# The first 512-token chunk of an attention-and-MLP kernel: ScalarE's first instructions, VectorE's and ScalarE's orders, and TensorE's first products rearranged

## The chip, the cores and the metric

One core of a Trainium2 chip runs the kernel. The metric is device microseconds of that core for one launch. The core has TensorE (PE in the profile; its weight loads are PEld), VectorE (DVE), ScalarE (ACT), GpSimd (POOL) and SyncE (SP), which issues most of the transfers. SP and ACT each have a transfer queue of their own (q1 and q10 in the profile); all queues share 16 DMA engines.

## What is computed

The input x has 2048 tokens of 1024 features, in bfloat16. It is normalised per token, goes through a dilated local attention (32 heads of 32, 8 keys at a distance of 2) and through a gated MLP with 3584 hidden features, and the two are combined:

```python
xn = _layernorm(x, axis=-1)
s = _A_ref(xn, A_wqkv, A_wo)      # qkv = xn @ wqkv; 8 keys at distance 2; softmax; @ wo
g = _silu(_B_ref(xn, B_w1, B_w3, B_w2))   # (silu(xn @ w1) * (xn @ w3)) @ w2
return x + s * g
```

## The kernel before

Tokens are worked in four chunks of 512 (c = 0 to 3), two chunks to a block (b = 0, 1); a chunk has four rows of 128 tokens (st = 0 to 3). The products of a block are done by a Strassen-like scheme of seven products on halves of the two chunks and halves of the features, so that sums of inputs and of weights on VectorE take the place of some products on TensorE.

**A planner orders everything but TensorE.** The kernel's body only records operations in a `Plan`: engine, name, what is read and written, an estimated duration. TensorE's operations stay in the order in which they are recorded. For the other engines `simulate` (L130) runs a list schedule with those estimates: whenever an engine is free it takes, of the operations ready by then, the one with the smallest `limit`. `limits` (L109) derives that from when TensorE needs the result; `plan.soon` lowers it by name; `plan.rank` replaces it by a fixed place for named operations of the start. The instructions are then emitted in the order found. Each engine runs its own in that order, and real waits are by semaphore. A transfer's estimate goes through one pipe with `plan.rate` bytes per microsecond, whatever queue issues it.

**The start.** Ahead of the plan, 19 products on a tile of zeros (`warm`, L296) are queued on TensorE, each 128x512. Then, for chunk 0:

- `x_load` (L371) brings the four rows of x, 256 KB each: rows 0 and 1 are issued by SP, rows 2 and 3 by ACT (names x0_0 to x0_3). SP goes on with wqkv0_0 and wqkv0_1 (two halves of the query weights, 1 MB each), four rows of chunk 1, and wqkv1_0, wqkv1_1.
- "warm" on ACT (L1155) is a square root on a dummy, so that its function table is loaded early.
- `ln_dve` (L379) normalises rows 0, 1 and 3 on VectorE: two statistics (bn0_0_0, bn0_0_1 for row 0, L385), their merge (ba0_0, L388), a square root on ACT (sq0_0, L390), a reciprocal on VectorE (rc0_0, L392) and the scaling (ts0_0, L393). `ln_act` (L397) normalises row 2 on ACT: mean0_2 (L404), var0_2 (L409), sq0 (L413), then rc0 and nm0 on VectorE (L416, L417), then nrm0_2 (L421).
- `ln_tp` (L425) transposes a normalised row on TensorE by eight products with an identity, four for each half of the features (L434), and an eviction brings each half from PSUM to `xT` (L441; xT0_0_0 and xT0_0_1 are the halves of row 0). All evictions of chunk 0 are on ACT.
- `qkv_first` (L518) with `rows0` (L1179) makes the first query products as soon as a row is there: for each row 16 products of 128 columns on wqkv0_0 and the first half of that row's features (L311). They need xT0_st_0 alone. `fill` (L1171) puts products on zeros into the order to bridge a wait; they write a bank that the first products of row 0 overwrite.

TensorE's order at the start is: transposes of row 0; fill of 5; transposes of row 1; products of row 0; transposes of row 2; products of row 1; transposes of row 3; products of row 2; products of row 3. After that come `fsnap`, copies of the four banks by ACT, and 16 products on wqkv0_1 and the second halves (called fc11 here, from the name of their evictions), then the same for the key weights, between which the rows of chunk 1 are transposed (tp1_0 to tp1_3).

Chunk 1's normalisation (bn1_0_0 and so on) is ranked behind chunk 0's. `attention` (L615) of a chunk runs on VectorE, beside the MLP's products: logits into E; transfers L of E; sums z; maximum and sum trees tr; zd; exp on ACT; rec; pb; transfers E back; then the weighted sum of values. For chunk 3 alone `plan.soon` lowers the limits of L, z, tr, zd, exp, rec, pb and E by 200 us.

Of the kernel before, what the change touches and what calls it, by code (L numbers as in the profile page):

```python
# [14 lines left out]
PE, DVE, ACT, POOL, SP = range(5)  # L15
# [14 lines left out]

class Op:
    __slots__ = ("eng", "emit", "rd", "wr", "occ", "lat", "table", "nbytes", "pred", "succ", "n",
                 "start", "done", "ready", "limit", "name", "late", "idx", "rate")


class Plan:
# [3 lines left out]
    def __init__(self):  # L40
        self.ops, self.slots, self.pools = [], [], {}
        self.shift = 0.0
        self.rate = 3e5
        self.rank, self.soon = {}, {}

    def slot(self, pool, name):
        s = Slot(self, pool, name)
# [1 line left out]
        self.slots.append(s)  # L49
        return s  # L50

    def op(self, eng, name, emit, rd=(), wr=(), occ=0.0, lat=0.08, table=None, nbytes=0, late=0.0):
        o = Op()
        o.eng, o.name, o.emit, o.rd, o.wr, o.occ, o.lat = eng, name, emit, list(rd), list(wr), occ, lat
        o.table, o.nbytes, o.late, o.idx, o.rate = table, nbytes, late + self.shift, len(self.ops), self.rate
        for c in o.rd + o.wr:
            s = c[0] if isinstance(c, tuple) else c
            if isinstance(s, Slot):
                if s.first is None:
                    s.first = o.idx  # L60
                s.last = o.idx
        self.ops.append(o)
        return o
# [45 lines left out]
    def limits(self):  # L109
        t = 0.0  # L110
        for o in self.ops:
            o.limit = None
            if o.eng == PE:
                o.limit = t
                t += o.occ
        for o in reversed(self.ops):
            lim = [self.ops[s].limit - self.hop(o, self.ops[s]) for s in o.succ]
            lim = min(lim) if lim else t
            d = o.occ + o.lat
            if o.nbytes:  # L120
                d = o.occ + 2.6 + o.nbytes / o.rate
            lim -= d
            o.limit = lim if o.limit is None else min(o.limit, lim)
            o.limit += o.late
        for o in self.ops:
            o.limit += self.soon.get(o.name, 0.0)
            if o.name in self.rank:
                o.limit = self.rank[o.name] - 1000.0

    def simulate(self):  # L130
        ops = self.ops
        free = [0.0] * 5
        ready = [[] for _ in range(5)]
        pes = [o.idx for o in ops if o.eng == PE]
        pe_at = 0
        table = None
        pipe = 0.0
        for o in ops:
            o.n, o.ready = len(o.pred), 0.0
            o.start = None  # L140
        for o in ops:
            if not o.n:
                ready[o.eng].append(o.idx)
        left = len(ops)
        order = []
        while left:
            best = None
            for e in reversed(range(5)):
                if e == PE:
                    if pe_at == len(pes) or ops[pes[pe_at]].n:  # L150
                        continue
                    T = max(free[PE], ops[pes[pe_at]].ready)
                elif ready[e]:
                    T = max(free[e], min(ops[i].ready for i in ready[e]))
                else:
                    continue
                if best is None or T < best[0]:
                    best = T, e
            T, e = best
            if e == PE:  # L160
                o = ops[pes[pe_at]]
                pe_at += 1
            else:
                i = min((i for i in ready[e] if ops[i].ready <= T), key=lambda i: (ops[i].limit, i))
                ready[e].remove(i)
                o = ops[i]

            occ = o.occ
            if o.table and o.table != table:
                occ += 1.29  # L170
                table = o.table
            o.start = T
            free[e] = T + occ
            if o.nbytes:
                pipe = max(pipe, T + occ + 0.9) + o.nbytes / o.rate
                o.done = pipe + 1.3
            else:
                o.done = T + occ + o.lat
            left -= 1
            order.append(o)  # L180
            for s in o.succ:
                q = ops[s]
                q.n -= 1
                q.ready = max(q.ready, o.done + self.hop(o, q))
                if not q.n and q.eng != PE:
                    ready[q.eng].append(s)
        self.order = order
        return order
# [13 lines left out]
def kernel(  # L202
# [101 lines left out]
    def mm(ps, lhs, rhs, first, rd, last=True, mark=(), st=None):  # L304

        n = len(lhs)
        cut = (lambda a: a) if st is None else (lambda a: a[:, st * P:(st + 1) * P])

        def emit():
            for k in range(n):  # L310
                nc.tensor.matmul(  # L311
                    cut(ps.ap()), lhsT=lhs[k](), rhs=cut(rhs[k]()), start=(first and k == 0),
                    stop=(last and k == n - 1), skip_group_check=not (first and last) or st is not None,
                )

        plan.op(PE, "mm " + ps.name, emit, rd, [ps] + list(mark), n * (MM if st is None else TP), 0.0)
# [11 lines left out]
        plan.op(ACT, name, lambda: nc.scalar.activation(out=o(), in_=a(), func=ACTF.Silu), rd, wr, occ, 0.11,  # L328
                table="silu")

    def dma(eng, name, o, a, rd, wr, kb, late=0.0):
        e = {SP: nc.sync, POOL: nc.gpsimd, ACT: nc.scalar}[eng]
        occ = {SP: 0.45, POOL: 0.58, ACT: 0.55}[eng]
        plan.op(eng, name, lambda: e.dma_start(out=o(), in_=a()), rd, wr, occ, 0.0, nbytes=kb * 1024, late=late)  # L334

    def sub_of(s, *idx):
        return (s,) + idx
# [33 lines left out]
    def x_load(c, st, xt, eng=SP):  # L371
        g = c * NST + st
        dma(eng, f"x{c}_{st}", lambda: xt.ap().rearrange("p (s d) -> p s d", s=NST)[:, st, :],
            lambda: x_flat[g * P:(g + 1) * P, :], [], [(xt, st)], 256)

    def xrow(xt, st):
        return xt.ap().rearrange("p (s d) -> p s d", s=NST)[:, st, :]
# [85 lines left out]
    def qkv_w(wt, k, j):  # L463
        return lambda: wt.ap().rearrange("p (k c j) -> p k j c", k=4, j=NJ)[:, k, j, :]
# [53 lines left out]
    def qkv_first(nm, wts, mid=None, rows=None):  # L518

        pa = [bank(f"f{nm}{j}") for j in range(4)]  # L520
        for st in range(NST) if rows else ():
            rows(st, pa[0])
            for j in range(4):
                mm(pa[j], [qkv_w(wts[0], k, j) for k in range(KH)], bx[0, 0], st == 0, [wts[0]] + xt_cells(0, 0, st),
                   st=st)
        for j in range(4):
            if mid is not None and j != 2:
                mid(min(j, 2))
            if not rows:
                mm(pa[j], [qkv_w(wts[0], k, j) for k in range(KH)], bx[0, 0], True, [wts[0]] + xt_cells(0, 0))  # L530
            dst, wr = first_at(nm, j)
            cp("fsnap", dst, pa[j].ap, [pa[j]], wr)
        for j in range(4):
            if mid is not None and j == 0:
                mid(3)
            mm(pa[j], [qkv_w(wts[1], k, j) for k in range(KH)], bx[0, 1], False, [wts[1]] + xt_cells(0, 1))
            dst, wr = home(0, nm)(j)
            cp("fc11", dst, pa[j].ap, [pa[j]], wr)
# [609 lines left out]
        pend.append(tail)  # L1148


    x0, x1 = plan.slot("r8", "x0"), plan.slot("r8", "x1")
    plan.rate = 3.3e5
    for st in range(NST):
        x_load(0, st, x0, ACT if st > 1 else SP)
    plan.op(ACT, "warm", lambda: nc.scalar.activation(out=scr[:], in_=eps_t[:], func=ACTF.Sqrt), [], [], 0.2,  # L1155
            table="sqrt")
    plan.rank = {n: i for row in (
# [3 lines left out]
    ) for i, n in enumerate(row.split())}  # L1161
    for st in range(NST):
        for n in ("bn1_%d_0", "bn1_%d_1", "ba1_%d", "sq1_%d", "rc1_%d", "ts1_%d", "xT1_%d_0"):
            plan.rank[n % st] = len(plan.rank)
# [1 line left out]
    for st in range(NST):  # L1166
        if st == 2:
            ln_act(0, [2], x0)
        else:
            ln_dve(0, st, x0, [("seq", 0, 0)] if st == 1 else [])  # L1170
    def fill(ps, n):  # L1171

        def emit():
            for _ in range(n):
                nc.tensor.matmul(ps.ap(), lhsT=warm[:, 0:P], rhs=warm[:, 0:CH], start=True, stop=True)

        plan.op(PE, "fill", emit, [], [ps], n * MM, 0.0)

    def rows0(st, ps):  # L1179
        if st == 0:  # L1180
            ln_tp(0, 0, x0)
            fill(ps, 5)
            ln_tp(0, 1, x0)
        elif st < NST - 1:
            ln_tp(0, st + 1, x0, (ACT, ACT))

    plan.shift = 0.0
    for b in range(NB):
# [58 lines left out]
    attention(3)  # L1247
    wo(3, wots, last=t4_last)
    flush()
    plan.soon = {n + "3": -200.0 for n in ("L", "z", "tr", "zd", "exp", "rec", "pb", "E")}  # L1250
    plan.run()


# [28 lines left out]
```

## Time and profile before

| what | value |
|---|---|
| three runs | 720.35, 720.47, 720.61 us; median 720.47 |
| the profiled execution, its own time | 720.51 us |
| its span, first to last instruction | 718.7 us |
| what lies around the span | 1.8 us |
| PE busy | 710.5 us (99%), 3329 products |
| PEld, DVE, ACT, POOL busy | 344.6, 642.0, 385.6, 50.2 us |
| transfers | 150.55 MB, mean 209 GB/s |
| granted TensorE clock | 9 of 9 in all 40 slices |

The chain that ended last gives PE 98% of the span. "Busy" of PE counts the products on zeros too, and the end of each product is modelled: a 128x512 product is listed with 379 ns, while a stream of them starts every 0.216 us. Where rows are merged, the first number is the start of the first instruction, the second the time to the end of the last. A bracket at the end of a row is how long the engine had been idle, and what ended that.

### The profile page before, as it was taken

How to read it: one execution, taken by the hardware profiler on the slowest of the kernel's cores; microseconds unless marked ns; L12 is line 12 of the kernel's file. 1: busy time of each engine (PE TensorE's matmuls, PEld its weight loads, DVE VectorE, ACT ScalarE, POOL GpSimd, SP SyncE). 2: the span in 40 equal slices, each digit the busy share in tenths (PEclk: the TensorE clock that was granted, in tenths of full speed). 3: DMA queues.
4: the chain of work that ended last, by engine and by line, in shares of the span. 5: the costliest groups of instructions: out<-in, count | busy, mean ns of one | idle time of the engine just before them, and what ended most of it. 6: DMA issues, size and time to landing. Idle time of an engine off the chain costs nothing.

```text
span 718.7 us, 9254 instructions
## 1 busy us (share of the span) xinstructions
PE 710.5 (99%) x3329; PEld 344.6 (48%) x3384; DVE 642.0 (89%) x861; ACT 385.6 (54%) x655; POOL 50.2 (7%) x102
## 2 busy tenths in 40 slices
PE   9999999999999999999999999999999999999997
PEld 5655544444444444444555554444444444444443
DVE  6997999988999999589999999776999995899935
ACT  7754466576555799242535354676565654412133
POOL 0020100202000000202000000201000002200000
PEclk9999999999999999999999999999999999999999
DMA  9589895878644849884554559887537347655502
GB/s 337 191 293 387 285 335 162 265 204 242 210 138 165 287 148 227 247 243 122 186 164 157 175 197 318 266 292 236 185 114 252 111 155 213 212 196 171 175 30 88
DMA packets 128589, 150.55 MB, mean 209 GB/s; under 512 B 13856, under 2 KB 105504, under 8 KB 124192
## 3 DMA queue, kind: packets, MB, share of 16 engines
q1 hardware_dynamic: 113728, 121.13, 52.6%
q0 software_dynamic: 6080, 26.22, 10.4%
q10 hardware_dynamic: 8736, 2.62, 2.0%
q8 instruction: 26, 0.43, 0.3%
q14 instruction: 19, 0.16, 0.1%
HBM read 106.95 MB, written 32.51 MB: 194 GB/s over the span
## 4 chain that ended last, share of the span: by engine, by line
PE 98%; DVE 1%; DMA 0%; issue 0%; DVEq 0%
PE mm L311 97%; DVE small L385 1%; PE mm L434 0%; DMA r<-in_A_x_dram 0%; DVE xT L320 0%; DVE r L393 0%; DVE small L388 0%; DVE small L392 0%; DVEq L320 0%
## 5 line engine op out<-in xcount | busy, mean ns | idle before, releaser
L311 PEld LDWEIGHTS <-r 128*128 128x128 f16 (+1 forms) x2288 | 239.7, 107 | 243.5 <-issue 0.2
L311 PE MATMUL mm<-xs,r 128*128 128x512 f16 x1280 | 295.2, 379 | 0.0
L311 PE MATMUL mm<-xT,r 128*128 128x512 bf16 (+1 forms) x968 | 224.3, 369 | 2.1
L325 ACT COPY k<-mm 128x512 f32<-128x512 f32 x192 | 112.4, 587 | 93.0 <-PE mm L311 92.2
L311 PE MATMUL mm<-r,h_sb 128*128 128x512 bf16 (+1 forms) x694 | 153.1, 379 | 0.5
L311 PEld LDWEIGHTS <-h_sb 128*128 128x128 f16 (+1 forms) x800 | 78.2, 98 | 94.4
L325 ACT COPY mm<-mm 128x512 f32<-128x512 f32 x88 | 50.3, 574 | 70.7 <-PE mm L311 63.7
L320 DVE TENSOR_TENSOR a<-a,a 128x2048 bf16<-128x2048 bf16 (+1 forms) x72 | 87.7, 1218 | 0.3
L320 DVE TENSOR_TENSOR a<-qo,kT 128x2048 bf16<-128x2048 bf16 x64 | 77.3, 1218 | 1.4 <-ACT kT L325 1.3
L320 DVE TENSOR_TENSOR a<-E,vT 128x2048 bf16<-128x2048 bf16 x56 | 66.3, 1219 | 0.0
L320 DVE TENSOR_TENSOR k<-mm,k 128x512 f32<-128x512 f32 x72 | 48.1, 684 | 18.5 <-PE mm L311 18.2
L320 DVE TENSOR_TENSOR h_sb<-mm,k 128x512 bf16<-128x512 f32 x96 | 63.4, 683 | 0.7 <-PE mm L311 0.2
L328 ACT ACTIVATE k<-k 128x512 bf16<-128x512 f32 x56 | 34.9, 631 | 51.4 <-DVE k L320 51.4
L320 DVE TENSOR_TENSOR r<-r,r 128x1024 f16<-128x1024 f16 (+5 forms) x61 | 49.3, 816 | 4.3 <-DMA r<-in_A_wqkv_dram 4.0
L320 DVE TENSOR_TENSOR h_sb<-h_sb,k 128x1024 bf16<-128x1024 bf16 x56 | 37.1, 685 | 13.1 <-ACT k L325 13.1
L328 ACT ACTIVATE h_sb<-mm 128x512 bf16<-128x512 f32 x60 | 35.7, 599 | 21.2 <-PE mm L311 21.1
L320 DVE TENSOR_TENSOR a<-a 128x1024 bf16<-128x1024 bf16 (+4 forms) x60 | 38.0, 633 | 8.3 <-ACT a L669 4.4
L320 DVE TENSOR_TENSOR qo<-qo,a 128x2048 bf16<-128x2048 bf16 x32 | 39.0, 1218 | 0.0
L325 ACT CAST k<-mm 128x512 bf16<-128x512 f32 x56 | 32.5, 585 | 10.9 <-PE mm L311 10.8
L334 POOL DMA_DIRECT2D a<-E x32 | 16.7, 528 | 304.8 <-ACT k L325 126.1
L320 DVE TENSOR_TENSOR h_sb<-h_sb 128x512 f16<-128x512 bf16 (+1 forms) x72 | 37.2, 564 | 0.4 <-DMA h_sb<-in_B_w_dram 0.3
L320 DVE TENSOR_TENSOR r<-r 128x1024 f16<-128x1024 bf16 (+1 forms) x34 | 25.6, 776 | 0.0
(87 smaller groups left out, 395.9 us busy)
## 6 DMA issues: line engine op xcount, KB each, us to landing
r<-in_B_w_dram SPq DMA_DIRECT2D x42, 512.0 KB, 4.7
s_dram<-r POOLq DMA_DIRECT2D x14, 1024.0 KB, 5.1
r<-t_dram SPq DMA_DIRECT2D x16, 896.0 KB, 5.9
r<-s_dram SPq DMA_DIRECT2D x14, 1024.0 KB, 5.3
r<-in_A_wqkv_dram SPq DMA_DIRECT2D x12, 1024.0 KB, 6.6
r<-in_B_w_dram SPq DMA_DIRECT2D x12, 896.0 KB, 4.9
h_sb<-in_B_w_dram SPq DMA_DIRECT2D x14, 512.0 KB, 9.7
t_dram<-h_sb POOLq DMA_DIRECT2D x14, 512.0 KB, 6.8
```

The costliest lines, as they stand in the source:

```text
L311: nc.tensor.matmul(cut(ps.ap()), lhsT=lhs[k](), rhs=cut(rhs[k]()), start=(first and k == 0), stop=(last and k == n - 1), skip_group_check= ...
L320: plan.op(DVE, name, lambda: fn(out=o(), in0=a(), in1=b()), rd, wr, occ, 0.08, late=late)
L325: plan.op(ACT, name, lambda: nc.scalar.copy(out=o(), in_=a()), rd, wr, occ, 0.11)
L328: plan.op(ACT, name, lambda: nc.scalar.activation(out=o(), in_=a(), func=ACTF.Silu), rd, wr, occ, 0.11, table="silu")
L334: plan.op(eng, name, lambda: e.dma_start(out=o(), in_=a()), rd, wr, occ, 0.0, nbytes=kb * 1024, late=late)
L385: plan.op(DVE, f"bn{c}_{st}_{h}", lambda h=h: nc.vector.bn_stats(out=stats[:, h, :], in_=xrow(xt, st)[:, h * 512:(h + 1) * 512]), [(xt, st ...
```

## The change

Five things change. None touches the arithmetic: the added products are on a tile of zeros and are added to a bank that holds partial sums of row 0.

1. ACT's order starts with the table load and the dummy square root; rows 2 and 3 of x are issued behind it.
2. The orders of the start are given in full. A new list, `plan.chains`, makes each named operation wait in the schedule for the one ahead of it, for VectorE, ACT and SP; until now the names only ranked what was ready. The rows differ from the old ones: on VectorE each ts comes ahead of the next row's second statistic, and xT0_1_0 (the first half of row 1) is evicted there, ahead of rc0 and nm0; on ACT sq0_0 comes ahead of mean0_2, xT0_0_0 ahead of sq0_1 and var0_2, xT0_1_1 ahead of nrm0_2.
3. TensorE's order: transposes of row 0; fill of 3; products of row 0; transposes of row 1; fill of 4 (added to the bank, not overwriting it); products of row 1; transposes of rows 3 and 2; products of row 3; products of row 2.
4. The planner's estimates: the rate at the start is 3.7e5 instead of 3.3e5 bytes per microsecond, and a transfer issued by ACT is put in a pipe of its own (`side`) at half the rate.
5. `plan.soon` holds for chunk 1 too.

```diff
             o.start = T
             free[e] = T + occ
-            if o.nbytes:
+            if o.side:
+                side = max(side, T + occ + 0.9) + 2 * o.nbytes / o.rate
+                pipe += o.nbytes / o.rate
+                o.done = side + 1.3
+            elif o.nbytes:
                 pipe = max(pipe, T + occ + 0.9) + o.nbytes / o.rate
                 o.done = pipe + 1.3
...
-            for s in o.succ:
+            for s in o.succ + ([] if o.then is None else [o.then]):
                 q = ops[s]
                 q.n -= 1
-                q.ready = max(q.ready, o.done + self.hop(o, q))
+                q.ready = max(q.ready, free[e] if s == o.then and o.idx not in q.pred else o.done + self.hop(o, q))
...
-        for st in range(NST) if rows else ():
-            rows(st, pa[0])
+        for i, st in enumerate(ROW0 if rows else ()):
+            rows(i, pa[0])
             for j in range(4):
-                mm(pa[j], [qkv_w(wts[0], k, j) for k in range(KH)], bx[0, 0], st == 0, [wts[0]] + xt_cells(0, 0, st),
+                mm(pa[j], [qkv_w(wts[0], k, j) for k in range(KH)], bx[0, 0], i == 0, [wts[0]] + xt_cells(0, 0, st),
                    st=st)
...
+    ROW0, TPS, FILLS = (0, 1, 3, 2), ((0,), (1,), (3, 2), ()), (3, 4, 0, 0)
     x0, x1 = plan.slot("r8", "x0"), plan.slot("r8", "x1")
-    plan.rate = 3.3e5
+    plan.rate = 3.7e5
...
-    plan.rank = {n: i for row in (
-        "bn0_0_0 bn0_0_1 ba0_0 bn0_1_0 rc0_0 bn0_1_1 ts0_0 ba0_1 bn0_3_0 rc0_1 bn0_3_1 ts0_1 ba0_3 rc0 nm0 rc0_3 ts0_3",
-        "x0_2 x0_3 warm mean0_2 sq0_0 var0_2 sq0_1 sq0 sq0_3 xT0_0_0 xT0_0_1 nrm0_2 xT0_1_0 xT0_1_1 xT0_2_0 xT0_3_0 xT0_3_1 xT0_2_1",
-        "x0_0 x0_1 wqkv0_0 wqkv0_1 x1_0 x1_1 x1_2 x1_3 wqkv1_0 wqkv1_1",
-    ) for i, n in enumerate(row.split())}
+    plan.chains = [row.split() for row in (
+        "bn0_0_0 bn0_0_1 ba0_0 bn0_1_0 rc0_0 ts0_0 bn0_1_1 ba0_1 bn0_3_0 rc0_1 ts0_1 bn0_3_1 ba0_3 xT0_1_0 rc0 nm0 rc0_3 ts0_3",
+        "warm x0_2 x0_3 sq0_0 mean0_2 xT0_0_0 sq0_1 xT0_0_1 var0_2 sq0 sq0_3 xT0_1_1 nrm0_2 xT0_3_0 xT0_2_0 xT0_3_1 xT0_2_1",
+        "x0_0 x0_1 wqkv0_0 wqkv0_1 x1_0 x1_1 x1_2 x1_3 wqkv1_0 wqkv1_1")]
+    plan.rank = {n: i for row in plan.chains for i, n in enumerate(row)}
...
-    def fill(ps, n):
+    def fill(ps, n, first):
...
-                nc.tensor.matmul(ps.ap(), lhsT=warm[:, 0:P], rhs=warm[:, 0:CH], start=True, stop=True)
+                nc.tensor.matmul(ps.ap(), lhsT=warm[:, 0:P], rhs=warm[:, 0:CH], start=first, stop=first,
+                                 skip_group_check=not first)
...
-    def rows0(st, ps):
-        if st == 0:
-            ln_tp(0, 0, x0)
-            fill(ps, 5)
-            ln_tp(0, 1, x0)
-        elif st < NST - 1:
-            ln_tp(0, st + 1, x0, (ACT, ACT))
+    def rows0(i, ps):
+        for st in TPS[i]:
+            ln_tp(0, st, x0, (DVE if st == 1 else ACT, ACT))
+        if FILLS[i]:
+            fill(ps, FILLS[i], i == 0)
...
-    plan.soon = {n + "3": -200.0 for n in ("L", "z", "tr", "zd", "exp", "rec", "pb", "E")}
+    plan.soon = {n + c: -200.0 for c in "13" for n in ("L", "z", "tr", "zd", "exp", "rec", "pb", "E")}
```

More of the change, by code (lines that the diff above doesn't have):

```diff
@@ L32 @@
     __slots__ = ("eng", "emit", "rd", "wr", "occ", "lat", "table", "nbytes", "pred", "succ", "n",
-                 "start", "done", "ready", "limit", "name", "late", "idx", "rate")
+                 "start", "done", "ready", "limit", "name", "late", "idx", "rate", "side", "then")
 class Plan:
@@ L43, in __init__ @@
         self.rate = 3e5
-        self.rank, self.soon = {}, {}
+        self.rank, self.soon, self.chains = {}, {}, []
     def slot(self, pool, name):
@@ L50, in slot, with op @@
         return s
-    def op(self, eng, name, emit, rd=(), wr=(), occ=0.0, lat=0.08, table=None, nbytes=0, late=0.0):
+    def op(self, eng, name, emit, rd=(), wr=(), occ=0.0, lat=0.08, table=None, nbytes=0, late=0.0, side=False):
         o = Op()
+        o.side, o.then = side, None
         o.eng, o.name, o.emit, o.rd, o.wr, o.occ, o.lat = eng, name, emit, list(rd), list(wr), occ, lat
@@ L128, in limits @@
                 o.limit = self.rank[o.name] - 1000.0
+        at = {o.name: o for o in reversed(self.ops)}
+        for row in self.chains:
+            for a, b in zip(row[:-1], row[1:]):
+                at[a].then = at[b].idx
     def simulate(self):
@@ L136, in simulate @@
         table = None
-        pipe = 0.0
+        pipe = side = 0.0
         for o in ops:
@@ L140, in simulate @@
             o.start = None
+        for o in ops:
+            if o.then is not None:
+                ops[o.then].n += 1
         for o in ops:
@@ L329, in silu, with dma @@
                 table="silu")
-    def dma(eng, name, o, a, rd, wr, kb, late=0.0):
+    def dma(eng, name, o, a, rd, wr, kb, late=0.0, side=False):
         e = {SP: nc.sync, POOL: nc.gpsimd, ACT: nc.scalar}[eng]
         occ = {SP: 0.45, POOL: 0.58, ACT: 0.55}[eng]
-        plan.op(eng, name, lambda: e.dma_start(out=o(), in_=a()), rd, wr, occ, 0.0, nbytes=kb * 1024, late=late)
+        plan.op(eng, name, lambda: e.dma_start(out=o(), in_=a()), rd, wr, occ, 0.0, nbytes=kb * 1024, late=late, side=side)
     def sub_of(s, *idx):
@@ L373, in x_load @@
         dma(eng, f"x{c}_{st}", lambda: xt.ap().rearrange("p (s d) -> p s d", s=NST)[:, st, :],
-            lambda: x_flat[g * P:(g + 1) * P, :], [], [(xt, st)], 256)
+            lambda: x_flat[g * P:(g + 1) * P, :], [], [(xt, st)], 256, side=eng == ACT)
     def xrow(xt, st):
```

## The prediction

> **What bounds the kernel.** I read the page's engine row first, then the chain that ended last, then the timeline of the first 24 us by engine, then the transfers of that stretch. The page:
>
> ```profile
> PE 710.5 (99%) x3329; PEld 344.6 (48%) x3384; DVE 642.0 (89%) x861; ACT 385.6 (54%) x655; POOL 50.2 (7%) x102
> ```
>
> TensorE is busy 710.5 of 718.7 us. So nothing that shortens other engines' work pays unless it takes a wait out of TensorE's stream, and nearly all of that stream without a wait lies behind the start. The chain from 8.85 us:
>
> ```profile
> 8.85 0.46 DVE r L393
> 9.31 0.05 issue
> 9.35 0.62 PE mm L434 x8
> 9.97 0.99 PE mm L311 x16
> 10.96 0.62 PE mm L434 x8
> ...
> 15.31 0.05 issue
> 15.37 3.19 PE mm L311 x14
> 18.55 0.45 PE mm L434 x8
> 19.00 0.87 PE mm L311 x4
> 19.87 0.55 PE mm L434 x8
> ```
>
> From 9.35 us on the chain is TensorE's. Before that it is VectorE's normalising of rows 0 and 1 behind the x transfer, which suggests that an earlier x row would move all the rest. TensorE's own timeline says otherwise:
>
> ```profile
> 1.25 6.50 PE L296 MATMUL mm<-k 128*128 128x512 bf16 x19 [1.25 <-DVE k L294]
> 7.59 0.61 PE L434 MATMUL mm<-ident,r 128*128 128x128 bf16 x8
> 8.04 1.24 PE L1175 MATMUL mm<-k 128*128 128x512 bf16 x5
> 9.35 0.62 PE L434 MATMUL mm<-ident,r 128*128 128x128 bf16 x8
> ```
>
> The 19 products on zeros occupy it until 7.59, and row 0's transposes start right there. Row 0 was ready at 7.52 (ts0_0, 6.99 + 0.53). The change leaves the 19 as they are, so **7.59 is a floor**, however early x0_0 lands.
>
> **The budget from 7.59.** The next fixed point is the first product on wqkv0_1 (fc11), which ended at 15.31 and so started at 15.31 - 0.38 = 14.93. Between lie, before: 4 rows of transposes at 0.45 (7.59 to 8.04), 1.80; 5 fills at 0.216 (0.87 for four in the chain), 1.08; 64 products at 0.99/16, 3.96. That is 6.84 of 7.34 us. The 0.50 of waiting: 0.23 ahead of 9.35 (the fills end at 8.04 + 1.08 = 9.12), 0.16 ahead of 10.96 (16 products from 9.81 need 0.99, so 10.80; nrm0_2 ended at 9.67 + 1.24 = 10.91), some 0.11 ahead of fc11, which waits for the first fsnap copy (14.30 + 0.59).
>
> After: 7 fills, so work is 6.84 + 0.43 = 7.27. **Even if every wait of 0.50 went, the gain would be 0.07 us.** Now the waits.
>
> **Products of row 0** need row 0's first half, its eviction, and wqkv0_0. The rows:
>
> ```profile
> 1.67 1.28 ACT L1155 ACT_TABLE_LOAD   x1 [1.67 <-PEq L1266]
> 4.52 1.06 ACT L404 ACTIVATE r<-r 128x1024 bf16<-128x1024 bf16 x1 [1.35 <-DMA r<-in_A_x_dram]
> 8.02 1.07 ACT L441 CAST xT<-mm 128x512 bf16<-128x512 f32 x2
> 9.67 1.24 ACT L421 ACTIVATE r<-r,small 128x1024 bf16<-128x1024 bf16 x1
> ```
>
> xT0_0_0 runs 8.02 to 8.60 (1.07 for two with 0.59 each: they start 0.48 apart). The three fills end at 8.04 + 0.65 = 8.69. wqkv0_0, issued at 1.67, landed 6.8 later, at 8.5. So row 0's products start at 8.69, with no wait, and end at 9.68. Taking x0_2 and x0_3 out of the way does not bring wqkv0_0 sooner: the same 2 MB must move by then.
>
> **Row 1.** sq0_1 now stands behind xT0_0_0, so it starts at 8.50 and ends at 8.80 (0.29 in its row); rc0_1 (0.16) and ts0_1 (0.53, with the 0.03 between them) end near 9.55. Its transposes are free at 9.68: no wait, 0.1 to spare, to 10.13. The first half is in PSUM near 10.1 and xT0_1_0 goes to VectorE. The trace has no such copy there; the nearest rows are 0.42 (E<-a, 128x512 in SBUF) and 0.68 (an addition that reads PSUM, 128x512). I take 0.65, as the PSUM reader is nearer: done at 10.8, covered by the four fills to 10.99. At 0.42 nothing changes. Were the fills away, row 1's products would wait 0.7.
>
> **Rows 3 and 2.** Row 1's products end at 11.98, row 3's transposes at 12.43; ts0_3 (behind rc0, nm0, rc0_3) is done at 11.8. Row 2 hangs on ACT, from 8.50, by the spacing of starts: sq0_1 0.21, xT0_0_1 0.48, var0_2 1.04 and its read-out 0.21, sq0 0.21, sq0_3 0.21, xT0_1_1 0.48, which gives 11.35; nrm0_2 takes 1.24 and ends at 12.6. The transposes of row 2 therefore wait from 12.43 to 12.65: 0.2. The evictions and products behind them then follow closely, and fsnap ahead of fc11 keeps its 0.1. Sum: 7.27 + 0.2 + 0.1 = 7.57 against 7.34, **0.23 us later** at fc11.
>
> **Behind it** TensorE has one wait that may go: 0.10 ahead of tp1_1 (0.55 instead of 0.45 at 19.87), behind VectorE's ts1_1. There sq1_0 stands on ACT behind all the fsnap copies, and VectorE waited 1.47 us for it; the estimate for x1_0 is now earlier, so sq1_0 should move up. wqkv1_0 (landed 18.1 against 18.8 for its first product) sets no wait. I take half: -0.05. An order made worse there costs at most that 1.47 once more.
>
> **The x rows of ACT.** Load 1.28 and square root 0.20 from 0.74 put x0_2's issue at 2.25 and x0_3's at 2.7. With the delays of before (below) they land at 6.05 and 7.3. mean0_2 must start by 8.02 - 1.15 = 6.87 not to hold xT0_0_0; bn0_3_0, ahead of rc0_1, by 8.2. Both are met; if the issue is not held by the load at all, they land near 4.7, which is as good.
>
> ```profile
> r<-in_A_x_dram ACTq DMA_DIRECT2D x1, 256.0 KB, 3.8
> ...
> r<-in_A_x_dram ACTq DMA_DIRECT2D x1, 256.0 KB, 4.6
> ...
> q1 hardware_dynamic: 291, 0.53, 53.1%
> q10 hardware_dynamic: 272, 0.50, 50.2%
> ```
>
> The last two rows are of 2.6 to 5.2 us: ACT's queue got half of the bytes while both had work. The Trainium skill (DMA: Bandwidth & Descriptors, Issuing engines are not separate DMA queues) says that transfers from all issuers interleave on the same 16 engines and several issuers only save issue time; the trace agrees, and by that rule no order of queues gains anything for wqkv0_0. Another page speaks against the change: the Trainium skill (ScalarE: Activation LUTs, What ACT_TABLE_LOAD costs) counts a drain of about 1.38 us behind the load. The trace shows none (load to 2.96, square root at 2.97); by an estimate from that page x0_2 would land near 7.4 and the sum be 0.5 higher.
>
> **plan.soon for chunk 1, and every order replanned.** VectorE's softmax of chunk 1:
>
> ```profile
> 306.88 0.69 DVE L320 TENSOR_TENSOR k<-mm,k 128x512 f32<-128x512 f32 x1 [9.01 <-PE mm L311]
> 307.49 1.22 DVE L320 TENSOR_TENSOR a<-a 128x1024 f32<-128x1024 bf16 x1
> ```
>
> VectorE idled 9.01 us there behind a PSUM reader; z, tr and zd will now run in one block of some 6 us, ahead of three such readers. Their banks are wanted next by the products of wo near 340, 25 us on. Cost nothing; without that cover up to 6 us. Elsewhere TensorE shows no wait between 24 and 714 us, so a reorder can only lose: 0, with +1.5 as the upper bound.
>
> **Sum.** 0.23 - 0.05 = +0.18 on the profiled 720.51 (718.7 of span, 1.8 around it): 720.7. The median of the runs, 720.47, is 0.04 below the profiled one. About 0.2% (1.44 us) is what a measurement of this kernel can tell from no change; this is an eighth of it.
>
> **Rivals.**
>
> - *The waits all go* (ts0_3 and nrm0_2 sooner than I count, tp1_1 too): -0.07 - 0.10, 720.3. For it: the orders are full and x0_0 lands sooner. Against: ACT's chain from 8.50 is a sum of rows. 0.13.
> - *ACT is held by mean0_2*, slower than before: mean0_2 now stands ahead of xT0_0_0 and sq0_1, so a late x0_2 stops both rows. From a landing at 6.87 each microsecond costs one; if x0_2 only moved behind wqkv0_0, it would land at 8.5 + 0.65 = 9.1, xT0_0_0 start at 10.3 instead of 8.02, and the time be 723.0. For it: SP's queue is full by then, which it was not when the halves were measured. Against: the even shares. 0.10.
> - *A replanned order makes TensorE wait* near chunk 1's rows or the softmax: +0.5 to +1.5, 721.7. 0.10.
> - *The first transposes lead*, faster by over 1.44: it needs the floor at 7.59 to fall, which only a shorter run of the 19 could do. 0.04.
> - *The load does not hold ACT's issues*, so the change does not do that part: 720.7 all the same; it is inside the forecast.
>
> Forecast 0.63, own range 720.4 to 721.1. Down to 719.9 and up to 722.0 I leave out the fastest case, the full price of mean0_2 and some of the reorders. Faster 0.04; slower the 0.10 and a third of the reorders, 0.14; the rest, 0.82, within.
>
> **What would show it.** Row 0's transposes still at 7.59; row 0's products at 8.69; row 1's transposes at 9.7; a wait for nrm0_2 ahead of row 2's; fc11 near 15.2; q10's rows landing before 6.9 and 8.2. I am wrong if row 0's transposes start well before 7.59, if mean0_2 starts after 6.87, or if TensorE shows a new wait behind 24 us.

## The result, and the profile after

The changed kernel takes 722.84 us (median of 8 runs, 721.87 to 723.63) beside 720.66 (8 runs, 720.35 to 720.98): ratio 1.003, 95% interval 1.002 to 1.0039. It is slower by 2.2 us, and the interval lies clear of 1. The profiled execution took 723.34 us with a span of 721.2; before, 718.7.

The page's engine row and the first row of its chain:

```profile
PE 714.3 (99%) x3386; PEld 345.2 (48%) x3386; DVE 643.1 (89%) x862; ACT 384.5 (53%) x654; POOL 50.2 (7%) x102
...
PE 94%; DMA 2%; DVE 2%; issue 1%; ACT 0%; DVEq 0%; ACTq 0%
```

The first row hides the loss: PE is still at 99%, and its 3.8 us more of busy time are mostly 57 more recorded products, where the change adds two (some records were missing from the trace of before). The second row shows it: 94% of the chain is TensorE's, where it was 98%, and transfers are in it now.

TensorE's timeline of the start (start, time to the end of the last, engine, line, tiles, count, in brackets the idle time before):

```profile
1.25 6.83 PE L308 MATMUL mm<-k 128*128 128x512 bf16 x19 [1.25 <-DVE k L306]
7.92 0.61 PE L446 MATMUL mm<-ident,r 128*128 128x128 bf16 x8
8.37 0.81 PE L1188 MATMUL mm<-k 128*128 128x512 bf16 x3
9.01 1.14 PE L323 MATMUL mm<-xT,r 128*128 128x128 bf16 x16
9.99 0.61 PE L446 MATMUL mm<-ident,r 128*128 128x128 bf16 x8
10.44 1.03 PE L1188 MATMUL mm<-k 128*128 128x512 bf16 x4
11.35 1.15 PE L323 MATMUL mm<-xT,r 128*128 128x128 bf16 x16
12.34 1.20 PE L446 MATMUL mm<-ident,r 128*128 128x128 bf16 x16
13.40 2.88 PE L323 MATMUL mm<-xT,r 128*128 128x128 bf16 x35
```

The order is the new one, and little is idle in it: 0.13 ahead of row 2's transposes (which in the merged row begin at 12.92), 0.05 ahead of row 1's products and, as before, 0.1 ahead of fc11. fc11 starts at 15.48 instead of 14.94. Of these 0.54 us, 0.33 are the end of the 19 products on zeros (7.92 instead of 7.59), and 0.21 are the new order's own.

The rest of the loss is far behind the start. TensorE's timeline at 147 to 170 us:

```profile
147.00 2.75 PE L323 MATMUL mm<-xs,r 128*128 128x512 f16 x12
150.95 1.02 PE L323 MATMUL mm<-xs,r 128*128 128x512 f16 x4 [1.19 <-DVE h_sb L332]
...
167.35 1.89 PE L323 MATMUL mm<-xT,r 128*128 128x512 bf16 x8
169.69 1.89 PE L323 MATMUL mm<-xs,r 128*128 128x512 f16 x8 [0.45 <-ACT k L337]
```

Twelve products from 147.00 at 0.216 us end their turn at 149.59; the next starts at 150.95, **1.36 late**. Eight from 167.35 give 169.08, and the next starts at 169.69, **0.61 late**. (The brackets are smaller because the modelled end of a product lies 0.16 behind its turn.) From fc11 to the last product the trace has 699.41 us before and 701.36 after: +1.95, and these two waits are 1.97 of it. So 0.54 + 1.95 = 2.49 make the 2.5 us of span.

Who is late? VectorE's timeline, of the last reading of kT (the keys of chunk 0, in the buffer that chunk 1's are loaded into) and of the work ahead of the late product; SP's, which lists issues; and a row of the chain:

```profile
131.27 1.22 DVE L332 TENSOR_TENSOR a<-qo,kT 128x2048 bf16<-128x2048 bf16 x1
...
144.61 0.69 DVE L332 TENSOR_TENSOR h_sb<-mm,k 128x512 bf16<-128x512 f32 x1
149.60 0.69 DVE L332 TENSOR_TENSOR r<-r 128x1024 f16<-128x1024 bf16 x1 [4.29 <-DMA r<-in_B_w_dram]
150.21 0.68 DVE L332 TENSOR_TENSOR h_sb<-mm,k 128x512 bf16<-128x512 f32 x1
```

```profile
132.90 0.61 SPq L346 DMA_DIRECT2D kT<-park_k  x1
133.61 2.43 SPq L346 DMA_DIRECT2D r<-in_B_w_dram  x2
138.52 11.47 SPq L346 DMA_DIRECT2D a<-E  x8
```

```profile
134.29 15.21 DMA r<-in_B_w_dram
```

VectorE waited 4.29 us for a weight block of the MLP (w3.6, 512 KB), which SP issued at 134.29 and which landed at 149.5. The eviction at 150.21 stands behind that block in VectorE's order, and it is what TensorE's product at 150.95 waits for. With w1.6, w3.6 is queued behind `getk1`, the reload of 1 MB of keys into kT, and that may not start before VectorE's last reading (131.27 + 1.22 = 132.49) and a copy that ScalarE makes of kT's edge behind it (to 132.87). SP issues in order, so the two weights stood behind a transfer that could not go. The same rows of before:

```profile
129.39 3.82 SPq L334 DMA_DIRECT2D r<-in_B_w_dram  x2
136.59 0.61 SPq L334 DMA_DIRECT2D kT<-park_k  x1
```

There both weights went first, the second at 132.85, and they landed at 133.42 and 138.64. So w3.6 was issued 1.4 later than before and landed 10.9 later: most of its delay came in the queue, behind the keys and w1.6 and beside a store of 1 MB that POOL issued at 134.58. What SP's being held costs is seen in the stretch from 129 to 134 us (busy time of each engine, granted clock, share of the DMA engines' time, GB/s), after and then before:

```profile
129.00:134.00 5.00, 5.00 (x25) 2.25 (x23) 5.00 (x8) 2.35 (x5) 0.00 (x0) 1.00 0.00 0
```

```profile
129.00:134.00 5.00, 5.00 (x25) 2.29 (x24) 5.00 (x9) 1.34 (x3) 0.53 (x1) 1.00 0.61 210
```

For 5 us **no byte moves**, and then kT, both weights, a store and sixteen transfers of E go out together and finish near 150.

### The profile page after: what moved, and what is told of

Read it like the earlier page. It is cut to its first block, busy times and chain, and to the rows that moved or that the text cites. A ratio compares the mean times of both kernels' runs of the same rounds, so it can differ in the third digit from the quotient of the medians.

```text
span 721.2 us, 9319 instructions
## 1 busy us (share of the span) xinstructions
PE 714.3 (99%) x3386; PEld 345.2 (48%) x3386; DVE 643.1 (89%) x862; ACT 384.5 (53%) x654; POOL 50.2 (7%) x102
## 4 chain that ended last, share of the span: by engine, by line
PE 94%; DMA 2%; DVE 2%; issue 1%; ACT 0%; DVEq 0%; ACTq 0%
PE mm L323 93%; DMA r<-in_B_w_dram 2%; PE mm L308 1%; DVE a L332 1%; PE mm L446 1%; DVE r L332 0%; DVE h_sb L332 0%; ACT k L337 0%; PE mm L1188 0%; DVE k L332 0%; DVE xT L332 0%; ACT h_sb L340 0%; DVEq L332 0%; ACT L340 0%; DVE k L306 0%
## 5 line engine op out<-in xcount | busy, mean ns | idle before, releaser
L323 PE MATMUL mm<-xT,r 128*128 128x512 bf16 (+1 forms) x1008 | 227.4, 369 | 0.0
```

The source lines that it names most:

```text
L323: nc.tensor.matmul(cut(ps.ap()), lhsT=lhs[k](), rhs=cut(rhs[k]()), start=(first and k == 0), stop=(last and k == n - 1), skip_group_check= ...
```

## The experiments

Theory A: the loss is in the re-planned order behind the start, in its narrow form in `getk1` ahead of w1.6 and w3.6. Theory B: it is in the new start. Theory C: `plan.soon` for chunk 1. Where a kernel's orders are called pinned, the sequence of every engine but TensorE is written out as a list and nothing is planned. "Rest" is the time from the start of fc11 to that of the last product, 699.41 us before.

### The cost constant alone

```diff
 (before)
-    plan.rate = 3.3e5
+    plan.rate = 3.7e5
```

> The kernel before with one constant of the planner changed, 3.3e5 to 3.7e5 bytes per microsecond; the start keeps its instructions and SP's next orders differ. Theory A (the loss is an order: SP reloads kT ahead of the weights w1.6 and w3.6, the weights come late, TensorE waits near 150 us): the planner makes the same swap here, so slower than before by 1 to 2 us, 721.7 to 722.7, with a wait of TensorE of over 0.5 us between 145 and 172 us. Theory B (the loss comes from the new start itself): this kernel has none of the new start, 720.4 to 720.9. Theory C (the softmax of chunk 1 moved forward): also 720.4 to 720.9.

Measured: 724.73 us (722.25 to 725.38), ratio 1.005, interval 1.0038 to 1.0062. A number in the planner, which no instruction of the chip carries, costs more by itself than the whole change. But the place is another than expected. SP's timeline near 132 us, TensorE's at 325 to 358, and a row of the chain:

```profile
131.59 0.61 SPq L334 DMA_DIRECT2D kT<-park_k  x1
132.30 3.20 SPq L334 DMA_DIRECT2D r<-in_B_w_dram  x2
```

```profile
325.77 3.62 PE L311 MATMUL mm<-r,h_sb 128*128 128x512 f16 x16
330.49 10.74 PE L311 MATMUL mm<-r,h_sb 128*128 128x512 f16 x49 [1.10 <-DMA r<-t_dram]
...
351.45 1.89 PE L311 MATMUL mm<-xT,r 128*128 128x512 bf16 x8
355.64 1.92 PE L311 MATMUL mm<-xs,r 128*128 128x512 f16 x8 [2.31 <-DVE r L320]
```

```profile
322.01 8.44 DMA r<-t_dram
```

By the spacing TensorE starts 1.27 late at 330.49 and 2.46 late at 355.64, together 3.73; the rest is 703.08, +3.67. SP has the same swap near 132 us, `getk1` ahead of both weights, and **nothing waits for it**: kT came free 1.3 us sooner than in the changed kernel (131.59 instead of 132.90), POOL's store of 1 MB had gone ahead (130.34 instead of 134.58), and w3.6 landed at 142.16, in time for its sum on VectorE at 143.84. What costs is later. A reload of t is issued by SP at 322.01 (316.64 before) and takes 8.44 us, and at 355.64 VectorE had waited for wqkv weights that landed at 354.34. A in general is borne out; its narrow form isn't, since the swap is there and does no harm, and the size was underestimated twofold.

### Only `getk1` moved back

```diff
 (after, orders pinned) SP:
-    w1.5 w3.5 getk1 w1.6 w3.6 L0
+    w1.5 w3.5 w1.6 w3.6 getk1 L0
```

> The changed kernel with every order of VectorE, ScalarE, GpSimd and SyncE kept as the planner had made it, but one transfer moved: the reload of kT stands behind w1.6 and w3.6 instead of ahead of them. Theory A: w3.6 lands near 139 instead of 149.5 us, the waits at 151 and 170 us (1.35 and 0.61) go or shrink to under 0.3, and 720.9 to 721.3 remains, of which 0.4 is the start. Theory B or C: 722.3 to 723.2, as the changed kernel.

This is called the swap run below. Measured: 721.61 us (721.37 to 723.76; seven of nine executions below 722.3, two above 723.5), ratio 1.0019, interval 1.001 to 1.0028. The weights land at 133.86 and 137.56, and the waits at 151 and 170 us are gone, so in the changed kernel this one place in SP's order made both. The time is above the 720.9 to 721.3 that was expected. The profiled execution is one of the two long ones and shows what is next. TensorE, then VectorE:

```profile
351.07 1.89 PE L447 MATMUL mm<-xT,r 128*128 128x512 bf16 x8
354.59 1.92 PE L447 MATMUL mm<-xs,r 128*128 128x512 f16 x8 [1.63 <-DVE r L456]
```

```profile
345.83 1.23 DVE L456 TENSOR_TENSOR qo<-E,vT 128x2048 bf16<-128x2048 bf16 x1 [2.19 <-DMA E<-a]
...
348.71 2.35 DVE L456 TENSOR_TENSOR a<-E,vT 128x2048 bf16<-128x2048 bf16 x2
...
353.32 1.22 DVE L456 TENSOR_TENSOR r<-r,r 128x2048 f16<-128x2048 bf16 x1
```

VectorE waits 2.19 us for E to come back, then does chunk 1's weighted sum, and the sum of weights (353.32 + 1.22 = 354.54) that TensorE needs stands behind it: 1.79 late. So one move mends one place, and the re-planned order has a second one that the first had covered: in the changed kernel the same sum ends at 354.04, 0.4 ahead of its product, because TensorE is already 2 us late there.

### The new start with the old rest, and the reverse

```diff
 (after, orders pinned)
-    the planned sequences behind the start
+    before's sequences behind the start
```

> The new start (orders, TensorE's order, fills) with all that follows in the orders of the kernel before, given operation by operation. Theory A: only the start's own cost is left, 0.2 to 0.5 us, so 720.8 to 721.2, and no wait of TensorE between 35 and 714 us. Theory B: 722.3 to 723.2.

Measured: 720.84 us (720.56 to 721.59), ratio 1.0003, interval 0.9995 to 1.0012. No wait behind 35 us; rest 699.42, before's to 0.01. TensorE's start, and what the 19 products do to it:

```profile
1.25 5.93 PE L432 MATMUL mm<-k 128*128 128x512 bf16 x19 [1.25 <-DVE k L430]
7.02 0.61 PE L570 MATMUL mm<-ident,r 128*128 128x128 bf16 x8
7.46 0.81 PE L1312 MATMUL mm<-k 128*128 128x512 bf16 x3
8.69 1.20 PE L447 MATMUL mm<-xT,r 128*128 128x128 bf16 x16 [0.41 <-ACT xT L577]
```

The products on zeros end 0.9 earlier than in the profiled execution of the changed kernel, and 0.58 of it is given back ahead of row 0's products, which waited for wqkv0_0, landed at 8.64 (the bracket names an eviction that had ended at 8.02). fc11 starts at 15.14: +0.20. B falls: the whole start costs 0.1 to 0.2 us here.

```diff
 (before, orders pinned)
-    before's sequences behind the start
+    the changed kernel's sequences behind the start
```

> The start of the kernel before with all that follows in the orders of the changed kernel, given operation by operation (plan.soon has no part in it beyond the orders). Theory A: the waits at 151 and 170 us are there without the new start, so 722.0 to 722.8. Theory B: 720.4 to 720.9. Theory C: 722.0 to 722.8 too, but with the wait behind 300 us.

Measured: 723.36 us (721.57 to 723.53), ratio 1.0031, interval 1.0019 to 1.0042, with the waits at 151.19 (1.26) and 169.94 (0.61); rest 701.31. The loss goes with the rest. The start was not quite before's: ScalarE's list was the old row of ranks taken literally, with sq0_3 ahead of xT0_0_0, which put fc11 at 15.79. So 0.85 of this time is not the rest's, which is why it lies above the 722.0 to 722.8 expected, and the time stands only for where the waits are.

### `plan.soon` alone

```diff
 (before)
-    plan.soon = {n + "3": -200.0 for n in (...)}
+    plan.soon = {n + c: -200.0 for c in "13" for n in (...)}
```

> The kernel before with one edit: chunk 1's steps are also planned with "soon". Start, cost constant and everything else are before's; the planned orders differ from before's only in 42 places of VectorE's order, all behind 319 us. Theory A (the later planned order holds the weights, and "soon" is not what moved them): no wait of TensorE longer than 0.3 us behind 30 us, 720.4 to 721.0. Theory C ("soon" for chunk 1 is what costs): 721.7 or more, with a wait behind 300 us.

Measured: 720.82 us (720.49 to 721.07), ratio 1.0002, interval 0.9993 to 1.0011. No wait behind 300 us; one of 0.42 at 62 us, where the orders are the same as before's, so it belongs to the execution and not to the edit (the kernel with `getk1` first, below, has 0.40 there). C falls.

### The changed kernel with the old constant

```diff
 (after)
-    plan.rate = 3.7e5
+    plan.rate = 3.3e5
```

> The changed kernel with one edit undone: the planner's cost constant goes back from 3.7e5 to 3.3e5. The planned order of SP then has w1.6 and w3.6 ahead of the reload of kT again. If the constant is what made the harmful order: the waits at 151 and 170 us are gone and the time is 720.8 to 721.6, before's plus the start's +0.2 and up to 0.7 for what another order does behind 300 us. If the harm is in the start's order or in "soon": the waits stay, 722.3 to 723.2.

Measured: 720.96 us (720.69 to 721.61), ratio 1.0004, interval 0.9996 to 1.0013. Rest 699.32, no wait behind 31 us. The new start, the full lists and the pipe of their own for ACT's transfers are all still in, so none of them makes the loss. With the earlier runs this is a table of two by two:

| | 3.3e5 | 3.7e5 |
|---|---|---|
| old start, `soon` for chunk 3 | 720.7 | 724.73 |
| new start, `soon` for chunks 1 and 3 | 720.96 | 722.84 |

Nearly all of the loss stands in the column of 3.7e5, in both rows. Its size there differs by 1.9, with the order that comes out.

### `getk1` ahead of the weights in the kernel before

```diff
 (before, orders pinned) SP:
-    w1.5 w3.5 w1.6 w3.6 getk1 L0
+    w1.5 w3.5 getk1 w1.6 w3.6 L0
```

> The kernel before with every order pinned as it was, and one step moved on SP: the reload of kT (getk1) is issued ahead of w1.6 and w3.6 instead of behind them. If that one move is the cause of the waits at 151 and 170 us: kT's issue is held until VectorE has read the last logits (132 to 137 us), both weights go out some 4 to 8 us later than before, TensorE waits over 1 us in all between 145 and 172 us, 722 or more. If the move alone is harmless: no such wait, 720.4 to 721.0.

Measured: 728.63 us (727.28 to 728.81), ratio 1.0107, interval 1.0093 to 1.0121. VectorE, then TensorE, then the rows of the stretches 156 to 158 and 160 to 170 us (the granted clock is the third number from the end):

```profile
150.04 1.29 DVE L451 TENSOR_TENSOR r<-r 128x1024 f16<-128x1024 bf16 x2 [8.81 <-DMA r<-in_B_w_dram]
...
152.65 1.28 DVE L451 TENSOR_TENSOR k<-mm,k 128x512 f32<-128x512 f32 x2
153.84 1.28 DVE L451 TENSOR_TENSOR h_sb<-mm,k 128x512 bf16<-128x512 f32 x2
```

```profile
147.10 1.89 PE L442 MATMUL mm<-xs,r 128*128 128x512 f16 x8
154.58 3.57 PE L442 MATMUL mm<-xs,r 128*128 128x512 f16 x8 [5.59 <-DVE h_sb L451]
157.95 2.10 PE L442 MATMUL mm<-xT,r 128*128 128x512 bf16 x8
```

```profile
156.00:158.00 2.00, 2.00 (x7) 0.64 (x5) 1.97 (x3) 1.07 (x3) 0.00 (x0) 0.50 0.94 398
...
160.00:170.00 10.00, 10.00 (x48) 4.49 (x46) 9.56 (x17) 7.87 (x11) 0.34 (x1) 1.00 0.36 105
```

One step moved past two others in SP's order costs 8 us. In this order VectorE reads kT last from 135.79 to 137.01 and ScalarE's copy ends at 137.40, so SP is held until 137.43, the weights land at 146.65 and 149.94, and TensorE starts 5.75 late. Then the granted clock is 0.50 until about 158.4, for 3.8 us of work, and eight products take 3.37 us instead of 1.73, 1.64 more.

That this single move can make such a wait is shown; that it must is not, since under the cost constant alone it made none. Nor does the landing alone tell the size: w3.6 landed only 0.43 later than in the changed kernel (149.94 and 149.51), and TensorE waits 5.75 instead of 1.36. The rows lay the rest to VectorE's order, which no run changed alone. Here four evictions stand behind the sums of the weights (two at 152.65, two at 153.84), and TensorE goes on when the third is done, at 154.53. In the changed kernel three of the four had run ahead of that wait, the third at 144.61, and only the one at 150.21 stood behind.

### `getk1` on another queue

```diff
 (after, orders pinned)
-    getk1 on SP, ahead of w1.6
+    getk1 on POOL, ahead of s_dram#5
```

> The changed kernel with its orders pinned and one transfer moved to another queue: the reload of kT (getk1) is issued by POOL, ahead of its store s_dram#5, instead of by SP ahead of w1.6 and w3.6. It still waits for VectorE's last read of kT and is issued at about the same time (133 us); only SP is no longer held behind it. If the held queue is the cause: w1.6 and w3.6 go out near 130 and 133.5 us and land by 139, no wait of TensorE at 151 and 170, and the time is that of the swap run, 721.4 to 722.2 in most executions and over 723 in some, by the place at 354 us. If it is kT's megabyte that competes with the weights for the same engines: the weights still land late (after 143 us), the waits stay at 1 us or more in all, 722.3 to 723.5.

Measured: 721.84 us (721.07 to 723.25), ratio 1.0016, interval 1.0007 to 1.0026. SP and POOL:

```profile
129.82 3.82 SPq L470 DMA_DIRECT2D r<-in_B_w_dram  x2
```

```profile
133.06 0.91 POOL L470 DMA_DIRECT2D kT<-park_k  x1 [7.74 <-ACT kT L604]
```

The keys are issued at the time of the changed kernel (133.06 and 132.90), 0.2 us ahead of w3.6. Yet w3.6 lands at 137.34, 4.1 us behind its issue at 133.27, against 15.2 in the changed kernel, w1.6 lands at 133.66, and the waits at 151 and 170 us are gone. So it was the **held queue**, with the weights behind the megabyte in it, and not the megabyte as such. The Trainium skill (DMA: Bandwidth & Descriptors, Queues, rings and completion order) says that a DMA engine takes turns between queues and works through one queue in order; the runs agree: from 134 to 137.3 us SP's queue got 0.52 MB here and POOL's 0.32, and in the changed kernel SP's three landed in the order of their issue (139.22, 145.80, 149.51). What is left of the loss is 0.50 at fc11 and waits of 0.29 at 352.68 and 0.25 at 377.13.

### `soon` taken out, the swap kept

```diff
 (after, orders as planned with soon for chunk 3 alone, pinned) SP:
-    getk1 w1.6 w3.6
+    w1.6 w3.6 getk1
```

> The changed kernel with the order that the planner gives without "soon" for chunk 1, pinned, and the reload of kT moved behind w3.6 as in the swap run. If "soon" makes the weak place at 354 us that the swap run showed in some executions: no wait there, 720.8 to 721.3 in all executions. If the weak place comes from the re-planned order in general: as the swap run, 721.4 in most and over 723 in some, with a wait of 1 us or more between 300 and 360 us in those.

Measured: 723.12 us (722.58 to 723.8), ratio 1.0036, interval 1.0022 to 1.0049. There is no wait at 354 us, but at a fourth place:

```profile
700.29 1.02 PE L447 MATMUL mm<-h_sb,qo 128*128 128x512 f16 x4
702.03 1.02 PE L447 MATMUL mm<-h_sb,qo 128*128 128x512 f16 x4 [0.71 <-DVE r L456]
703.23 2.12 PE L447 MATMUL mm<-h_sb 128*128 128x512 f16 x9 [0.18 <-DVE h_sb L456]
```

0.88 and 0.34 late. VectorE was busy 29.69 us of the 30 up to 700 and so had little room; before it was busy 17.62 there, in the changed kernel 28.44, which sufficed. With `soon` for chunk 1 that place has no wait (the swap run, 721.61). The first half of the expectation was met, the second wasn't: without `soon` the wait at 354 goes, but another comes, and the time is longer by 1.5.

## Why the prediction was wrong

The time was 722.84, outside 719.9 to 722.0. The step that failed is "plan.soon for chunk 1, and every order replanned", in its last sentence: "a reorder can only lose: 0, with +1.5 as the upper bound". It measured **+1.95** in the rest of the profiled execution, and +3.67 with the constant alone. So the term was put at nothing because no wait was seen, and what the runs showed in its place is a transfer that SP held ahead of two weights: two waits, 1.36 and 0.61, that go when it is moved back. They are also the sign of error that the prediction named, a new wait behind 24 us. The mechanism stood among the rivals as "A replanned order makes TensorE wait", 721.7 with a chance of 0.10. The sign and the kind were right, the chance far too low, the upper end of +1.5 half a microsecond too small, and the place was neither chunk 1's rows nor the softmax but SP's queue. The error of thought: a TensorE without waits between 24 and 714 us was read as slack. It says only that this order has none; the 8 us for one step moved in SP's order show how little stands behind it. And I looked at VectorE's order alone.

The swap can be followed in the planner's source. `plan.rate` holds for the first twelve transfers only, those of x and wqkv at the start (at L1200 of the kernel before it goes back to 3e5), but everything later is scheduled from where they end. And `simulate` takes what is ready first, however late its limit. In the kernel before it reckons, in the plan's own time, w1.6 ready at 132.78 us and `getk1` at 135.50; in the changed kernel 132.21 and 130.45. So `getk1`, whose limit is 353, goes ahead of w1.6, whose limit is 144. On the chip it was the other way round: w1.6 could go at 130.07 (the swap run), `getk1` not before 132.87.

Point by point:

- *The floor at the end of the 19 products*: right as a mechanism, wrong as a number. x0_0 landed at 4.06 instead of 4.31 and it gained nothing. But the products on zeros ended anywhere from 7.02 to 8.06 us in kernels that have them alike, so that the floor can fall with no shorter run of them, which the prediction had ruled out. It then meets wqkv0_0 at 8.6 to 8.8 (above).
- *The budget to fc11, +0.23*: right. Measured against the floor of the same execution it is +0.21 (15.48 - 14.94 - 0.33); the new start with the old rest shows +0.20, and 0.14 in the medians. Row by row, with 0.33 taken off: row 0's products at 8.68 (8.69 was said), row 1's transposes at 9.66 (9.68), the wait for nrm0_2 0.13 (0.2). VectorE's eviction of row 1, taken as 0.65 from the nearest reader of PSUM, took 0.64.
- *Behind it, -0.05*: by 24.2 us the lag is 0.44, so 0.10 was won back.
- *ScalarE's x rows*: the condition was met, the course was the other one named. ScalarE's timeline:

```profile
0.74 1.28 ACT L1168 ACT_TABLE_LOAD   x1 [0.74 <-PEq L1278]
0.91 0.88 ACTq L346 DMA_DIRECT2D r<-in_A_x_dram  x2
2.03 0.20 ACT L1168 ACTIVATE scr<-eps_t 128x1 f32<-128x1 f32 x1
```

  The issues stand behind the load in the order and yet go at 0.91 and 1.34, during it. The rows landed at 4.71 and 6.07, before at 4.50 and 5.75: with the load ahead of them they came 0.2 to 0.3 later. The rival in which mean0_2 holds ACT did not come about: mean0_2 started at 5.86, and 6.87 was the limit. The Trainium skill (ScalarE: Activation LUTs, What ACT_TABLE_LOAD costs) adds some 1.38 us of drain to the load; the square root starts 0.01 behind it here, as before.
- *`plan.soon`, nothing*: right for the kernel before (720.82 beside 720.7); under the new constant, with the swap, the kernel is 1.5 us longer without it.

Two things stay open. One is why the same pinned order takes 721.4 in most executions and 723.5 in some (the swap run): only a profile of the long kind was seen. The other is how twelve estimates at the start bring VectorE's last reading of kT forward by 5 us in the plan (from 133.83 to 128.78).

No version beat the kernel before: the three nearest, 720.82, 720.84 and 720.96, have intervals that hold 1.

## What to carry to other kernels

A constant in a scheduler's cost model is an edit to the whole program: when it is touched, compare the emitted orders of every queue, and cost each step that passes another. In a queue that issues in order, a transfer that must wait for a reader belongs behind those that could go, or on another queue; look for a stretch where the DMA share falls to 0.00 with work outstanding. Such a stretch is a sign and not yet a cost: under the constant alone nothing moved from 129 to 131 us either, and TensorE did not wait for it. What stands behind the late data in the order of the engine that reads it decides how much is lost. And an engine that never waits tells nothing of how far it is from waiting.

## What was unexpected of the hardware

- **The end of the 19 products moves by 1 us between executions**: row 0's transposes, with nothing else to wait for, started at 7.02, 7.17, 7.59 and six times between 7.90 and 8.06 us in nine kernels (in the other two they waited for VectorE), because the full clock is granted at another product: from 4.64 us on in the first of these, from 6.75 in the last. The Trainium skill (TensorE: Matmul & The Clock Gate, What's actually happening) says that the window in which activity is judged runs free of the kernel's start, so that the change varies by half a microsecond to either side; here it varies by 2.1 us in all, which is more.
- **A wait of 5.59 us costs the clock, one of 2.31 doesn't**: in the first, 0.50 was granted from about 151.5 to 158.4 us, 3.8 us into the work behind it; behind the second, eight products took 1.76 us, in a stream 1.73. The Trainium skill (TensorE: Matmul & The Clock Gate, What's actually happening) has the clock fall after an idle window of about 3.4 us, which lies between the two.
- **A table load doesn't hold ScalarE's own issue of transfers**: 0.91 us, with the load from 0.74 to 2.02.
